# Walking the columns of float32r matmuls in steps of four 16-byte lines, with operands moved to other start addresses

## The chip, the cores and the metric

The kernel runs on one core of a Trainium2 chip. The metric is the device time of one execution in microseconds (us). Three runs of the kernel before gave 803.9, 803.96 and 804.22 us; the median is 803.96 us.

## What is computed

The reference is an attention with a sigmoid in place of the softmax, followed by a channel mix:

```python
scores = scale * np.matmul(q, k.transpose(0, 1, 3, 2)) - np.log(S)
attn = 1.0 / (1.0 + np.exp(-scores))
x = np.matmul(attn, v)                       # then laid out as [batch, seq, 768]
x_prev = x shifted by one position, zeros first
xk = mu_k * x + (1.0 - mu_k) * x_prev
xr = mu_r * x + (1.0 - mu_r) * x_prev
k = np.maximum(xk @ w_k, 0.0)
out = sigmoid(xr @ w_r) * ((k * k) @ w_v)
```

There are 8 batches, 12 heads of 64 dimensions, 448 positions, 768 channels and 1024 hidden channels. The inputs are float32, some of the weights float64.

## The kernel before, in words

**Number formats.** TensorE multiplies float32 as it is, or as float32r, a shorter form that streams one column a cycle. Where the kernel uses float32r it splits each operand into a rounded part (hi) and the remainder (lo) and adds three products, hi by hi, lo by hi and hi by lo, in PSUM. ScalarE or VectorE makes the hi part by a copy, VectorE the lo part by a subtraction.

**Attention** (the first 246 us) walks over 48 pairs of heads, two pairs to a round. For each pair and each 128-row chunk of keys, `scores` (line 348) issues the three float32r products (`kh`, `kl` are the keys, `qh`, `ql` the queries), each as two matmuls, one for each head of the pair, in the upper and the lower 64 rows of the array (line 361). The keys are the stationary operand, whose weights are loaded, and the queries the moving operand, whose 448 columns are streamed. The very first chunk is done in plain float32. `score_tails` (line 372) does the last 64 keys in float32, in four 64x64 tiles of the array at once. `sigmoid` (line 383) takes the scores out of PSUM on ScalarE. `weigh` (line 395) and its relatives multiply by the values in float32, also in four 64x64 tiles (lines 402 and 426), and `gather` (line 432) makes the two mixes of x and writes them to DRAM.

**Channel mix** (from 246 us to the end) has three stages, R_ (w_r), K_ (w_k) and V_ (w_v). Each is a Strassen-like scheme of seven products in place of eight, over four sets of columns (`PAIRS`, line 562): three of 512 columns and one of 256. `convert_seven` (line 269) has made the seven combinations of the weights from float64 on VectorE while attention ran; they stand in `slots`, hi and lo. `operand` (line 587) makes the hi and lo parts of the moving operands, in the tiles `rr` and, reused from attention, `qh` and `ql`. `multiply` (line 646) issues the products, with line 670 as the one matmul instruction; every matmul loads 128 columns of weights of its own and streams 512 or 256 columns into one PSUM bank. `evacuate` and `finish` take the results out.

**Order of the work.** A planner (`Plan`, line 24) lists all operations with an engine, an assumed cost and a priority, simulates the engines, and writes the instructions out in the order of the simulated starts. DMAs go out on SyncE's queue, a few on ScalarE's.

**Addresses.** SBUF tiles are laid out one behind the other by `ring` (line 174), and `gap` (line 177) leaves bytes free between them. Per partition, counted from a multiple of 256 bytes: `slots`, `rr`, and everything behind them up to `wexpo` start at 224; `kn` and `vn` at 160; `qn`, `qh` and `ql` at 224; `kh` and `kl` at 160; `pf` and all behind it at 224. So the weights of the scores start 64 bytes lower than the queries that stream past them, and the weights of the products (pieces of 512 bytes of `slots`) at the same distance from a multiple of 256 as the streams.

Of the kernel before, what the change touches and what calls it, by code (L numbers as in the profile page):

```python
# [23 lines left out]
class Plan:  # L24
# [9 lines left out]
    def op(self, engine, cost, prio, run, reads, writes, dma=None, gate=False, opens=None):  # L34
        i = len(self.ops)
        deps = set()
        for r in reads:
            if r in self.writer:
                deps.add(self.writer[r])
        for w in writes:  # L40
            if w in self.writer:
                deps.add(self.writer[w])
            deps.update(self.readers.get(w, ()))
        for r in reads:
            self.readers.setdefault(r, []).append(i)
        for w in writes:
            self.writer[w] = i
            self.readers[w] = []
        deps.discard(i)
        self.ops.append(Op(engine, cost, prio, run, deps, dma, gate, opens))  # L50
# [58 lines left out]
def attention_then_channel_mix(  # L109
# [15 lines left out]
    nc = tc.nc  # L125
    P = 128
# [40 lines left out]
    WK_PACE, WV_PACE = 1.5, 1.5  # L167
    CAST_DVE = lambda n, a: n % 2 == 1 or n == 2

    WHOLE = 1  # L170
    ZEROS = 336
    Q_FIRST = 256

    def ring(pool, name, bufs, shape, dtype):
        return [pool.tile(shape, dtype, name=f"{name}{i}") for i in range(bufs)]

    def gap(pool, name, size):
        pool.tile([P, size // 4], F32, name=name)

    base = ctx.enter_context(tc.tile_pool(name="base", bufs=1, side="left"))  # L180
    apool = ctx.enter_context(tc.tile_pool(name="apool", bufs=1, side="right"))
# [2 lines left out]
    pscore = psc.enter_context(tc.tile_pool(name="pscore", bufs=1, space=PSUM, side="right"))  # L184

    slots = ring(base, "slot", 7, [P, 2 * WO], F32R)
    rr = ring(base, "rr", 6, [P, 2, T], F32R)
    ys = ring(base, "ys", 3, [P, T], F32)
    wraw = ring(base, "wraw", 2, [P, WP, 2], U32)
# [5 lines left out]
    vnr = ring(apool, "vn", 5, [P, T], F32)  # L195
    gap(apool, "gap1", 64)
    qnr = ring(apool, "qn", RAW, [P, T], F32)
    qhr = ring(apool, "qh", LEAD, [P, T], F32R)
    qlr = ring(apool, "ql", LEAD, [P, T], F32R)
    gap(apool, "gap2", 192)  # L200
    kh = ring(apool, "kh", LEAD, [P, KW], F32R)
    kl = ring(apool, "kl", LEAD, [P, KW], F32R)
    gap(apool, "gap3", 64)
    pfr = ring(apool, "pf", PFB, [P, 2, T], F32)
    ptr = ring(apool, "pt", PTB, [P, 2, T], F32)
    xxr = ring(apool, "xx", 2, [P, T], F32)
# [8 lines left out]
    sc = ring(pscore, "sc", 3, [P, 2, 512], F32)  # L215
# [8 lines left out]
    def mm(n, cols):  # L224
        return n * (cols / 2.4 + 13.4)

    def act(n, sbuf=False, ptr=False):
        return 100 + 0.834 * n + 42 * sbuf + 93 * ptr

    def dve(n, fast=False, ptr=False):  # L230
        return 135 + n / (1.92 if fast else 0.96) + 61 * ptr
# [37 lines left out]
    def convert_seven(w, t, half_rows, n, pace, at, put):  # L269
# [32 lines left out]
        combine(sub, s4, a12, s2, at + 3 * pace)  # L302
        put(2, s4, at + 3 * pace)

    def to_slot(t, n):
        def put(p, a, at):
            g = POS[p]
            hi, lo = (slots[g][:, half * KT[R_] * n + t * n:half * KT[R_] * n + (t + 1) * n] for half in range(2))
            K = ("slot", g, t)
            op(ACT, act(n, True), at, lambda: nc.scalar.copy(hi, a[0]), [a[1]], [K], gate=True)  # L310
            op(DVE, dve(n), at, lambda: nc.vector.tensor_sub(lo, a[0], hi), [a[1], K], [K + ("lo",)])
        return put
# [18 lines left out]
    def prepare(n, at):  # L331
        i = n % LEAD
        k0 = WHOLE * P if n == 0 else 0
        for src, hi, lo, a, w in ((kn[n % RAW][:, k0:KW], [t[:, k0:] for t in kh], [t[:, k0:] for t in kl], "k", KW - k0), (qn[n % RAW], qh, ql, "q", S)):
# [6 lines left out]
    half = [slice(h * D, (h + 1) * D) for h in range(2)]  # L341

    def pe(cost, go, reads, writes, at, opens=None):
        op(PE, cost, at, go, reads, writes + ["order"], opens=opens)
# [3 lines left out]
    def scores(n, c, u, at):  # L348
        i, m = n % LEAD, n % RAW
        mark = (n, c) in ((N - 1, 1), (N - 2, 2), (N - 1, 2))  # L350
        if n == 0 and c < WHOLE:
            pairs, cost, reads = ((knr[m], qnr[m]),), 752, [("kn", m), ("qn", m)]
        else:
            pairs, cost = ((kh[i], qhr[i]), (kl[i], qhr[i]), (kh[i], qlr[i])), 602
            reads = [(a, i) for a in ("kh", "kl", "qh", "ql")]

        def go(lo, hi):
            for e, (kk, qq) in enumerate(pairs):
                for h in range(2):
                    w = T if mark and e == len(pairs) - 1 else hi  # L360
                    nc.tensor.matmul(sc[u][:, h, lo:w], kk[half[h], c * P:(c + 1) * P], qq[half[h], lo:w], start=e == 0, stop=e == len(pairs) - 1, skip_group_check=mark)  # L361

        keys = [("sc", u, 0), ("sc", u, 1)]
        if (n, c) == (0, 0):

            pe(cost * Q_FIRST / S, lambda: go(0, Q_FIRST), reads, keys, at)
            pe(cost * (1 - Q_FIRST / S), lambda: go(Q_FIRST, S), reads + [("qn", 0, 1)], keys, at)
            return
        pe(cost + 2 * SWITCH * (n % 2 == c == 0), lambda: go(0, S), reads, keys, at)
# [91 lines left out]
    for t in range(KT[R_]):  # L461
        convert_seven(w_r, t, KT[R_], CW[R_], WR_PACE, WR_FROM + 4 * WR_PACE * t + 0.4, to_slot(t, CW[R_]))
# [68 lines left out]
    e = N % RAW  # L531
# [109 lines left out]
    def slot_keys(g):  # L641
        return [("slot", g, h) + x for h in range(3) for x in ((), ("lo",))]
# [3 lines left out]
    def multiply(stage, s, p, i, at, cols=slice(0, T), b=None, turn=0):  # L646
        g = POS[p]
        b = b or (yb if p in (5, 6, 3) else xb)[i]
        c = cols.stop - cols.start
        rs_ = used[stage, s, p]  # L650
        w = CW[stage]
        small = PAIRS[s][1] < T

        def go():
            n = len(rs_)

            def left(t, a):
                return slots[g][:, a * n * w + t * w + i * P:a * n * w + t * w + (i + 1) * P]

            if small:  # L660

                a = turn ^ (p in (1, 6, 3))
                terms = [(left(t, a), r[0], (T, SMALL)[a]) for t, r in enumerate(rs_)]
            else:
                terms = [(left(t, a), r[e][:, cols], c) for t, r in enumerate(rs_) for a, e in ((0, 0), (0, 1), (1, 0))]
            for e, (l, r, m) in enumerate(terms):
                nc.tensor.matmul(b[0][:, :m], l, r[:, :m], start=bool(p in (0, 4) and e == turn == 0), stop=e == len(terms) - 1 and bool(turn or not small), skip_group_check=True)  # L670

        cost = mm(len(rs_), (T, SMALL)[turn ^ (p in (1, 6, 3))]) if small else mm(3 * len(rs_), c)
        op(PE, cost, at, go, [k for r in rs_ for k in r[2:]] + slot_keys(g), [b[1]])
# [87 lines left out]
    for step, (stage, s, p) in enumerate(steps):  # L761
# [6 lines left out]
        small = PAIRS[s][1] < T  # L768
        for i in range(rows if small else 0):
            multiply(stage, s, p, i, at + unit * i / (2 * rows))  # L770
        for i in range(rows):
# [9 lines left out]
            if step == len(steps) - 3 and i == rows - 1:  # L781
                a, b = yb[i], yb[NFH - 1]
# [45 lines left out]
```

## Time and profile before

| | |
|---|---|
| median of three runs | 803.96 us |
| span of the profiled execution, first to last instruction | 801.9 us |
| TensorE matmul busy | 797.8 us, 99% |
| TensorE weight loads busy | 598.8 us, 75% |
| VectorE busy | 639.7 us, 80% |
| ScalarE busy | 496.0 us, 62% |
| mean DMA rate | 224 GB/s |

The span is that of one profiled execution; the runs' times, taken without a profile, are 2.1 us above it at the median. In the profile PE is TensorE's matmuls, PEld its weight loads, DVE VectorE, ACT ScalarE, POOL GpSimd. Matmuls follow each other in a pipeline, and the duration listed for one reaches into the next ones; the distance between two starts is what one of them takes of the time. In the timeline equal instructions that follow each other are merged into one row, with their number behind the x.

### The profile page before, as it was taken

The page shows a single profiled execution, that of the slowest core. Times are in us where ns is not written, and L with a number is a line of the kernel's source. Part 1 is how long each engine was busy: PE and PEld are TensorE (multiplying, and loading weights), DVE is VectorE, ACT ScalarE, POOL GpSimd, SP SyncE. Part 2 cuts the span into 40 slices and gives each one's busy share as a digit, 9 for nine tenths or more (in the row PEclk, how much of TensorE's full clock was granted, in tenths as well). Part 3 has the DMA queues.
Part 4 walks back from the last instruction along what each step waited for, and adds up shares of the span by engine and source line. Part 5 has one row for each costly group of instructions (what it writes and reads, how often), then busy time and mean ns, then how long its engine had stood idle before and what let it go on. Part 6 is the DMA issues. An engine that isn't in the chain of part 4 may idle for free.

```text
span 801.9 us, 14343 instructions
## 1 busy us (share of the span) xinstructions
PE 797.8 (99%) x4935; PEld 598.8 (75%) x4935; DVE 639.7 (80%) x1210; ACT 496.0 (62%) x870; POOL 2.9 (0%) x33
## 2 busy tenths in 40 slices
PE   9999999999999999999999999999999999999998
PEld 5555555555556888888888888888888888888887
DVE  4889888898898998899987974668597585677955
ACT  6788888877785555568766464567773434345431
POOL 0000000000000000000000000000000000000000
PEclk9999999999999999999999999999999999999999
DMA  8977978789887967668877772445775564457505
GB/s 276 282 262 243 304 242 275 254 274 340 295 293 272 313 236 218 228 238 257 277 243 223 243 256 87 162 151 155 226 243 179 172 184 131 132 166 253 186 23 176
DMA packets 105336, 179.74 MB, mean 224 GB/s; under 512 B 11952, under 2 KB 58800, under 8 KB 105264
## 3 DMA queue, kind: packets, MB, share of 16 engines
q1 hardware_dynamic: 104976, 178.61, 68.9%
q8 instruction: 39, 0.64, 0.3%
q14 instruction: 33, 0.27, 0.1%
q10 hardware_dynamic: 288, 0.23, 0.1%
HBM read 109.06 MB, written 69.73 MB: 223 GB/s over the span
## 4 chain that ended last, share of the span: by engine, by line
PE 99%; DVE 0%; issue 0%
PE pb L670 69%; PE av L402 13%; PE sc L361 10%; PE sc L376 2%; PE av L426 2%; PE av L361 2%; PE av L412 1%; PE sc L445 0%; DVE vn L720 0%
## 5 line engine op out<-in xcount | busy, mean ns | idle before, releaser
L670 PE MATMUL pb<-rr,slot 128*128 128x512 f32 (+1 forms) x1908 | 440.3, 379 | 0.0
L670 PEld LDWEIGHTS pb<-rr,slot 128*128 128x128 f32 x1908 | 348.0, 188 | 68.5 <-issue 0.8
L670 PE MATMUL pb<-qh,slot 128*128 128x512 f32 (+1 forms) x468 | 154.7, 374 | 0.0
L402 PE MATMUL av<-pf,vn 64*64 64x448 f32 x1104 | 118.1, 540 | 0.0
L391 ACT ACTIVATE pf<-sc 128x896 f32<-128x896 f32 x120 | 104.0, 962 | 0.5 <-PE sc L361 0.5
L670 PEld LDWEIGHTS pb<-qh,slot 128*128 128x128 f32 x468 | 86.2, 188 | 15.8
L402 PEld LDWEIGHTS av<-pf,vn 64*64 64x64 f32 x1104 | 41.4, 132 | 56.9 <-issue 36.1
L670 PE MATMUL pb<-ql,slot 128*128 128x512 f32 (+1 forms) x177 | 68.4, 387 | 0.0
L594 ACT CAST rr<-ys 128x512 fp32r<-128x512 f32 (+1 forms) x56 | 30.9, 568 | 35.7 <-PE pb L670 34.1
L361 PE MATMUL sc<-qh,kh 64*128 64x448 f32 x238 | 46.2, 384 | 0.0
L728 ACT COPY pb<-pb 128x512 f32<-128x512 f32 x40 | 22.6, 575 | 34.5 <-PE pb L670 31.5
L361 PE MATMUL sc<-ql,kh 64*128 64x448 f32 (+1 forms) x238 | 43.4, 361 | 0.0
L436 ACT COPY xx<-av 128x448 f32<-128x448 f32 x48 | 23.3, 539 | 32.3 <-PE av L402 26.5
L361 PE MATMUL sc<-qh,kl 64*128 64x448 f32 x238 | 43.2, 359 | 0.0
L437 DVE TENSOR_TENSOR dx<-xx 128x448 f32<-128x448 f32 x48 | 29.9, 623 | 16.6 <-ACT xx L436 16.4
L595 DVE TENSOR_TENSOR rr<-pf,rr 128x512 fp32r<-128x512 f32 (+1 forms) x40 | 23.0, 608 | 20.5 <-ACT rr L594 20.5
L670 PEld LDWEIGHTS pb<-ql,slot 128*128 128x128 f32 x177 | 33.2, 188 | 6.7
L595 DVE TENSOR_TENSOR rr<-ys,rr 128x512 fp32r<-128x512 f32 (+1 forms) x56 | 33.6, 620 | 3.4 <-ACT rr L594 3.1
L361 PEld LDWEIGHTS sc<-qh,kh 64*128 64x128 f32 x238 | 22.4, 185 | 18.5 <-issue 15.5
L595 DVE TENSOR_TENSOR rr<-vn,rr 128x512 fp32r<-128x512 f32 (+1 forms) x48 | 29.6, 626 | 7.7 <-ACT rr L594 7.4
L594 ACT CAST rr<-vn 128x512 fp32r<-128x512 f32 (+1 forms) x48 | 26.9, 571 | 10.4 <-PE pb L670 8.8
L639 DVE TENSOR_TENSOR slot<-pf,slot 128x768 fp32r<-128x768 f32 x28 | 26.8, 956 | 7.8 <-ACT slot L638 7.6
(160 smaller groups left out, 1071.8 us busy)
## 6 DMA issues: line engine op xcount, KB each, us to landing
vn<-in_v SPq DMA_DIRECT2D x48, 224.0 KB, 4.3
xr_d<-mr SPq DMA_DIRECT2D x48, 224.0 KB, 4.5
xk_d<-mk SPq DMA_DIRECT2D x48, 224.0 KB, 4.3
kn<-in_k SPq DMA_DIRECT2D x47, 224.0 KB, 3.9
qn<-in_q SPq DMA_DIRECT2D x47, 224.0 KB, 4.2
wraw<-in_moe_w_k SPq DMA_DIRECT2D x12, 512.0 KB, 5.8
wraw<-in_moe_w_v SPq DMA_DIRECT2D x16, 384.0 KB, 3.7
k_d<-pt SPq DMA_DIRECT2D x23, 256.0 KB, 3.1
```

The costliest lines, as they stand in the source:

```text
L361: nc.tensor.matmul(sc[u][:, h, lo:w], kk[half[h], c * P:(c + 1) * P], qq[half[h], lo:w], start=e == 0, stop=e == len(pairs) - 1, skip_grou ...
L376: nc.tensor.matmul(sc[u][half[m % 2], h, :S], kn[m % RAW][half[h], KW:], qn[m % RAW][half[h], :], start=True, stop=True)
L391: op(ACT, 815, at, lambda: nc.scalar.activation(f, sc[u][:, :, :S], AF.Sigmoid, bias=NEG_LOG_S, scale=SCALE), R, K, opens=opens)
L402: nc.tensor.matmul(av[m % 2][half[h], :w], vn[m % 5][half[r], h * NC + c, :], pfr[(m * NC + c) % PFB][half[r], h, :w], start=(turn, c) == ...
L426: nc.tensor.matmul(av[r][half[h], :w], vn[(n + h) % 5][half[r], 2 * NC, :], ptr[n // 2 % PTB][half[r], h, :w], start=False, stop=stop, ski ...
L436: op(ACT, act(S), at - 1, lambda: nc.scalar.copy(x[:, 1:], av[n % 2][:, :S]), [AV[n % 2]], [X])
L437: op(DVE, dve(S), at, lambda: nc.vector.tensor_sub(d, x[:, 1:], x[:, :S]), [X], [G])
L594: op(ACT, act(w, True), at, lambda: nc.scalar.copy(hi, y[:, :w]), [Y], [H], gate=True)
L595: op(DVE, dve(w), at, lambda: nc.vector.tensor_sub(lo, y[:, :w], hi), [Y, H], [L])
L639: op(DVE, dve(n), at, lambda hi=hi, lo=lo, w=w: nc.vector.tensor_sub(lo, w, hi), W + [K], [K + ("lo",)])
L670: nc.tensor.matmul(b[0][:, :m], l, r[:, :m], start=bool(p in (0, 4) and e == turn == 0), stop=e == len(terms) - 1 and bool(turn or not sma ...
L728: op(ACT, act(T), at, lambda: nc.scalar.copy(y(), x()), [X], [Y])
```

## The change

Every float32r matmul of line 361 and all of line 670 get another order of columns. A new helper, `by_lines`, rearranges the free dimension of an operand of n columns, seen as n/16 blocks of four lines of four columns, so that the first lines of all blocks come first, then the second lines, and so on. A line is four float32 columns, 16 bytes. The moving operand and the PSUM output of a matmul are rearranged alike, so each column's result lands where it did before. In the instruction a read of 512 consecutive columns becomes one of 4 times 32 runs of 4 columns. Weights are read as before. The float32 matmuls (the first chunk of scores, the tails and the products with the values) are not touched.

Gaps move four groups of tiles. `rr`, `ys` and the tiles of the weight conversion move from 224 to 0 bytes past a multiple of 256, `qh` and `ql` as well, and `kh` and `kl` from 160 to 224. `slots`, `kn`, `vn`, `qn`, `pf` and all behind `pf` stay. So in scores and in products the weights now start 32 bytes below a multiple of 256, and the streams on one.

The planner's costs are not touched, and every engine's instructions stand in the order of before.

```diff
--- before.py
+++ after.py
@@ -167,6 +167,7 @@
     WK_PACE, WV_PACE = 1.5, 1.5
     CAST_DVE = lambda n, a: n % 2 == 1 or n == 2
 
+    LINE = 4
     WHOLE = 1
     ZEROS = 336
     Q_FIRST = 256
@@ -184,6 +185,7 @@
     pscore = psc.enter_context(tc.tile_pool(name="pscore", bufs=1, space=PSUM, side="right"))
 
     slots = ring(base, "slot", 7, [P, 2 * WO], F32R)
+    gap(base, "gap0", 32)
     rr = ring(base, "rr", 6, [P, 2, T], F32R)
     ys = ring(base, "ys", 3, [P, T], F32)
     wraw = ring(base, "wraw", 2, [P, WP, 2], U32)
@@ -195,12 +197,12 @@
     vnr = ring(apool, "vn", 5, [P, T], F32)
     gap(apool, "gap1", 64)
     qnr = ring(apool, "qn", RAW, [P, T], F32)
+    gap(apool, "gap5", 32)
     qhr = ring(apool, "qh", LEAD, [P, T], F32R)
     qlr = ring(apool, "ql", LEAD, [P, T], F32R)
-    gap(apool, "gap2", 192)
+    gap(apool, "gap2", 224)
     kh = ring(apool, "kh", LEAD, [P, KW], F32R)
     kl = ring(apool, "kl", LEAD, [P, KW], F32R)
-    gap(apool, "gap3", 64)
     pfr = ring(apool, "pf", PFB, [P, 2, T], F32)
     ptr = ring(apool, "pt", PTB, [P, 2, T], F32)
     xxr = ring(apool, "xx", 2, [P, T], F32)
@@ -302,6 +304,9 @@
         combine(sub, s4, a12, s2, at + 3 * pace)
         put(2, s4, at + 3 * pace)
 
+    def by_lines(t):
+        return t.rearrange("p (a b c) -> p b a c", b=4, c=LINE)
+
     def to_slot(t, n):
         def put(p, a, at):
             g = POS[p]
@@ -358,7 +363,10 @@
             for e, (kk, qq) in enumerate(pairs):
                 for h in range(2):
                     w = T if mark and e == len(pairs) - 1 else hi
-                    nc.tensor.matmul(sc[u][:, h, lo:w], kk[half[h], c * P:(c + 1) * P], qq[half[h], lo:w], start=e == 0, stop=e == len(pairs) - 1, skip_group_check=mark)
+                    out_, right_ = sc[u][:, h, lo:w], qq[half[h], lo:w]
+                    if len(pairs) > 1:
+                        out_, right_ = by_lines(out_), by_lines(right_)
+                    nc.tensor.matmul(out_, kk[half[h], c * P:(c + 1) * P], right_, start=e == 0, stop=e == len(pairs) - 1, skip_group_check=mark)
 
         keys = [("sc", u, 0), ("sc", u, 1)]
         if (n, c) == (0, 0):
@@ -667,7 +675,7 @@
             else:
                 terms = [(left(t, a), r[e][:, cols], c) for t, r in enumerate(rs_) for a, e in ((0, 0), (0, 1), (1, 0))]
             for e, (l, r, m) in enumerate(terms):
-                nc.tensor.matmul(b[0][:, :m], l, r[:, :m], start=bool(p in (0, 4) and e == turn == 0), stop=e == len(terms) - 1 and bool(turn or not small), skip_group_check=True)
+                nc.tensor.matmul(by_lines(b[0][:, :m]), l, by_lines(r[:, :m]), start=bool(p in (0, 4) and e == turn == 0), stop=e == len(terms) - 1 and bool(turn or not small), skip_group_check=True)
 
         cost = mm(len(rs_), (T, SMALL)[turn ^ (p in (1, 6, 3))]) if small else mm(3 * len(rs_), c)
         op(PE, cost, at, go, [k for r in rs_ for k in r[2:]] + slot_keys(g), [b[1]])
```

## Rows read from the trace of the kernel before

**Rows 1.** Page, parts 1 and 2: span; busy us, share, instructions; granted clock in tenths, 40 slices.

```profile
span 801.9 us, 14343 instructions
PE 797.8 (99%) x4935; PEld 598.8 (75%) x4935; DVE 639.7 (80%) x1210; ACT 496.0 (62%) x870; POOL 2.9 (0%) x33
...
PEclk9999999999999999999999999999999999999999
```

**Rows 2.** Page, part 4: the chain that ended last, by engine and line.

```profile
PE 99%; DVE 0%; issue 0%
PE pb L670 69%; PE av L402 13%; PE sc L361 10%; PE sc L376 2%; PE av L426 2%; PE av L361 2%; PE av L412 1%; PE sc L445 0%; DVE vn L720 0%
```

**Rows 3.** Waits, engine PE: releaser; us in total, times, longest.

```profile
PE sc L445 <- PEq L798: 0.8, 1, 0.8
```

**Rows 4.** Chain in order of time: start us, us, what.

```profile
246.29 552.32 PE pb L670 x2553
```

**Rows 5.** Groups by form, PE, whole span: count | busy us, mean ns | idle before.

```profile
L670 PE MATMUL pb<-rr,slot 128*128 128x512 f32 x1722 | 414.0, 389 | 0.0
L670 PE MATMUL pb<-qh,slot 128*128 128x512 f32 x403 | 141.3, 389 | 0.0
...
L670 PE MATMUL pb<-ql,slot 128*128 128x512 f32 x173 | 67.3, 389 | 0.0
...
L670 PE MATMUL pb<-rr,slot 128*128 128x256 f32 x186 | 29.3, 283 | 0.0
...
L670 PE MATMUL pb<-qh,slot 128*128 128x256 f32 x65 | 13.8, 283 | 0.0
...
L670 PE MATMUL pb<-ql,slot 128*128 128x256 f32 x4 | 1.1, 283 | 0.0
```

**Rows 6.** Timeline, PE and PEld, 300 to 304 us: start us, length us, what.

```profile
299.66 4.70 PE L670 MATMUL pb<-rr,slot 128*128 128x512 f32 x20
...
299.89 4.27 PEld L670 LDWEIGHTS pb<-rr,slot 128*128 128x128 f32 x19
```

**Rows 7.** Timeline, PE and PEld, 796.2 to 799 us.

```profile
796.27 0.28 PE L670 MATMUL pb<-qh,slot 128*128 128x256 f32 x1
...
796.99 0.88 PE L670 MATMUL pb<-rr,slot 128*128 128x256 f32 x6
797.71 0.28 PE L670 MATMUL pb<-qh,slot 128*128 128x256 f32 x1
...
797.71 0.19 PEld L670 LDWEIGHTS pb<-ql,slot 128*128 128x128 f32 x1
```

**Rows 8.** Timeline, PE, 53.2 to 57.5 us: scores of one pair.

```profile
56.62 0.36 PE L361 MATMUL sc<-qh,kl 64*128 64x448 f32 x2
...
57.42 0.36 PE L361 MATMUL sc<-ql,kh 64*128 64x448 f32 x2
```

**Rows 9.** Timeline, PE, the same stretch: float32 products.

```profile
53.19 0.93 PE L376 MATMUL sc<-qn,kn 64*64 64x448 f32 x8
53.94 2.44 PE L402 MATMUL av<-pf,vn 64*64 64x448 f32 x24
```

**Rows 10.** Groups by form, PE, 338.4 to 338.55 us: 256 columns behind a 512.

```profile
L670 PE MATMUL pb<-qh,slot 128*128 128x256 f32 x2 | 0.4, 283 | 0.0
L670 PE MATMUL pb<-rr,slot 128*128 128x256 f32 x1 | 0.3, 277 | 0.0
```

**Rows 11.** Groups by form, PE, 338.6 to 338.8 us: 512 columns behind two 256s.

```profile
L670 PE MATMUL pb<-rr,slot 128*128 128x512 f32 x1 | 0.4, 396 | 0.0
```

**Rows 12.** Groups by form, PE, 798.5 to 799 us: the last matmul.

```profile
L670 PE MATMUL pb<-qh,slot 128*128 128x256 f32 x1 | 0.3, 279 | 0.0
```

**Rows 13.** Windows: stretch, length, busy us (x) of PE, PEld, DVE, ACT, POOL; PEclk, DMA share, GB/s.

```profile
50.00:100.00 50.00, 49.97 (x500) 27.97 (x500) 44.72 (x93) 40.89 (x63) 0.49 (x5) 1.00 0.83 270
250.00:450.00 200.00, 200.00 (x912) 166.63 (x911) 178.55 (x326) 125.15 (x237) 0.00 (x0) 1.00 0.76 249
```

## The prediction

> **What bounds the kernel now.** I read the busy shares and the granted clock first. TensorE is busy for 797.8 of 801.9 us and its clock stands at the top digit in all 40 slices [rows 1]; the stage rows give 1.00, so the engine is at the upper of its two levels, 2.4 GHz. The chain that ended last is TensorE for 99%, and 69% of the span is the products of line 670 [rows 2]. TensorE's own waits come to 0.8 us, all at the start [rows 3]. In the chain in order of time the products are one unbroken piece of 552.32 us [rows 4]. So nothing that another engine does is on the path: the time is the number of matmuls by the time from the start of one to the start of the next. A matmul's listed duration (379 ns and the like) overlaps its neighbours and is no price. I read prices from the timeline, as distances between starts.
>
> *Products.* 2298 of them have 512 columns and 255 have 256 [rows 5]. Twenty of 512 columns in a row fill 4.70 us; without the last one's 0.39 that is 19 steps in 4.31 us, 226.8 ns a step [rows 6]. At 2.4 GHz and one column a cycle 512 columns are 213.3 ns, so 13.5 are over. From 796.27 to 797.71 us there are twelve of 256 columns: 120.0 ns a step, over 106.7, again 13.3 over [rows 7]. **The excess belongs to the matmul, not to its columns.** Over the whole stretch: 2298 x 213.33 + 255 x 106.67 = 517.4 us, 552.3 - 517.4 = 34.9, or 13.7 ns for each of 2553.
>
> *Scores in float32r.* Two 64-row matmuls run side by side; four pairs start between 56.62 and 57.42 us, 200 ns a pair against 186.7 for 448 columns: 13.3 over [rows 8]. There are 858 such matmuls, 429 pairs: 5.7 us. *Plain float32 products* (lines 376, 402) run four 64x64 tiles at once: 8 of them, two groups, from 53.19 to 53.94 us, 375 ns a group [rows 9]. That is 448 columns at two cycles each (373.3 ns) and under 2 ns over. **At half the reading pace the excess is all but gone, so it is no fixed price of changing weights.**
>
> *What the 13 ns go with.* A weight load is listed as 0.19 us and starts with the matmul before its own [rows 6, 7]. Beside 512 columns it lies inside one matmul; beside 256 columns its tail lies over its own. If loading slows streaming, the shares must shift where the two lengths meet, and they do. The first 256 after a 512, whose own weights were already in, lasts 277 ns where the next ones last 283 [rows 10]; the first 512 after 256s, which carries a tail as well as the next load, lasts 396 where 389 is usual [rows 6, 11]. The very last matmul has no load after it: 279 in place of 283 [rows 12]. The tail costs 6 to 7 ns, the head 4: about 10 ns of the 13.5 are paid while weights are read, and some 3.5 are left, near the float32 groups' 2.
>
> **The change, part by part.** *Order.* No instruction is added, removed or moved on any engine; counts, waits and DMAs stay. What changes is the order in which 2553 + 858 matmuls walk their columns, and four groups of addresses.
>
> *Moving operand, read as lines 0, 4, 8, ... and then 1, 5, 9, ...* All matmuls of the trace of before read consecutive columns, so it holds no price for this. Bounds: nothing gained (the conflict is one of capacity, every weight line costs a slot of the stream), or all 40.6 us (34.9 + 5.7). Between them stands the loads' measured share, 10 ns: if the reordered stream no longer meets the weights, 2553 x 10 + 429 x 10 = **29.8 us**. I take that value, as it rests on the rows nearest to the case: the same matmul with and without a load beside it [rows 10 to 12]. Why I think that the order can do it: two ascending streams of consecutive lines are read at once and delay each other by the same amount in products, where both start 224 bytes past a multiple of 256, and in scores, where the weights start 64 bytes lower. A shift of the start doesn't matter when both streams walk every line in turn; steps of four lines are another walk, in which they can keep out of each other's way. This is an inference; no row shows it.
>
> The rule that speaks against the change: the Trainium skill, "TensorE: Matmul & The Clock Gate", section "Step-by-step: what each phase is for", says that TensorE has two independent SBUF read ports, and that loading the next weights steals nothing from the running matmul's reads. By that rule the whole excess would be a fixed cost and the sum would be 0. The trace disagrees: 277, 283, 389 and 396 ns follow the loads.
>
> *Output, written in the same runs of four.* Nothing in the trace of before writes so. I cost it at 0; the far bound is a whole 2.4 GHz cycle for each of 128 runs (53.3 ns a product, see the rivals).
>
> *Addresses.* Slots stay 224 bytes past a multiple of 256; moving operands go to 0; keys of the scores go from 160 to 224, so that scores and products now have the same 32 bytes between weights and stream. With consecutive reading, products at distance 0 and scores at 64 pay 13.5 and 13.3 [rows 6, 8], so the shift alone is costed at 0; its bound is those 0.2 ns, 0.6 us either way. Scratch of the weight conversion moves by 32 bytes: 0, since no step waits for it [rows 3].
>
> *What a faster TensorE meets.* The closest cover is VectorE, with 178.55 of 200 us between 250 and 450 us [rows 13]. Products 10 ns shorter make that stretch about 191 us, and VectorE 93% busy. No capacity is exceeded, but operands come later relative to the matmuls. I charge **1 us** (bounds 0 and 3, a third of the stretch's 9 us). In attention VectorE does 44.72 of 50 us [rows 13], and TensorE gets only 4.3 us (429 x 10 ns) shorter over 240: nothing.
>
> *Sum.* 29.8 - 1 = 28.8 saved from 801.9: 773.1 us of span. The median of the runs is 803.96, 2.1 us above the span (execution outside it), so **775 us**.
>
> **The rivals.**
> *A. No change (within 0.2%, which is what a measurement of this kernel can tell from none: 1.6 us).* Weights and stream share something that one alone can use, whichever line it asks for. For: the excess is the same 13.3 to 13.7 ns at both distances and for 64-row pairs, as a fixed number of slots would be. Against: nothing, until other walks have been measured. 804 us.
> *B. Half of it.* Some lines still meet: 5 ns instead of 10 go, 14.9 us: 789 us. For: weights still pass every line. Faster too.
> *C. Slower: runs of four cost the output or the read a cycle each.* Place: the 128 run ends of each product (112 of a score). Price: 53.3 x 2298 + 26.7 x 255 + 46.7 x 429 = 149 us; with the 29.8 gained, 923 us. It decides from 10 / 128 = 0.08 ns a run, a fifth of a cycle: below that the change wins, and a whole cycle loses by far. For: every matmul in the trace writes consecutive columns, so it would not have shown. Against: with four columns to each line, as many lines are touched as before. The Trainium skill, "PSUM — Partial Sum Buffer", section "Specifications (TRN2)", says that any non-contiguous access slows matmuls significantly; its lines there are 8 bytes, of which each run fills two whole ones. No run here shows it yet.
> *D. Slower: the streams meet more often.* A step of 64 bytes repeats the same few places, and a load that falls into step with them is delayed at every line. Twice the share now: 10 ns more a matmul, 834 us. Against: the chosen 32 bytes between weights and stream differ from both distances of before.
>
> **How the numbers follow.** Forecast, the loads' share gone (from 8 to all 13.7 ns): 0.46. B: 0.17. Together faster by over 0.2%: 0.63. A: 0.17. C: 0.10 and D: 0.10, so slower: 0.20. The forecast's own range runs from all 40.6 us gone (763) to 8 ns with 3 us given back (783); little speaks for its low end, as float32 groups keep 2 ns: I cut at 766. To hold 8 in 10 the range must take in B and A: 766 to 806. C and D stay outside.
>
> **What would show it.** Right: a run of twenty 512-column products has steps near 216 to 218 ns, 256-column ones near 110, score pairs near 190; the products are one piece of about 527 us; durations no longer differ by 6 or 7 ns where 512 and 256 columns meet; no wait of TensorE over 1 us in 250 to 450. A: steps still 227. C: steps of 260 and more whether or not a load lies beside them. D: steps of 230 to 240, and a last matmul far shorter than its neighbours. Wrong in a way not listed: steps shorten, but TensorE begins to wait for operands.

## The result and the profile after

The changed kernel takes 795.41 us, the median of four runs (795.01 to 799.65), against 803.96 before: a ratio of 0.9909 with a 95% interval of 0.9885 to 0.9932. It is faster, by 8.5 us and not by the 28.8 that were forecast. The profiled execution is the slowest of the four, 799.65 us with a span of 797.5.

The page after, its head and the chain that ended last (before: [rows 1, 2]):

```profile
span 797.5 us, 14360 instructions
...
PE 793.1 (99%) x4935; PEld 598.8 (75%) x4935; DVE 639.3 (80%) x1210; ACT 495.9 (62%) x870; POOL 2.9 (0%) x33
...
PEclk9999999999999999999999999999999999999999
...
PE pb L678 68%; PE av L410 14%; PE sc L369 10%; PE sc L384 2%; PE av L434 2%; PE av L369 2%; PE av L420 1%; DMA qn<-in_q 0%; DVE vn L728 0%; ACTq L244 0%
```

TensorE bounds the kernel as before, at the same clock. Its chain in order of time, start and length in us, and pieces of the same chain in three stretches of some 60 and 30 us, where a row's length by its count is the mean step from one product to the next (the line is now 678):

```profile
1.16 3.58 DMA qn<-in_q
...
248.12 88.42 PE pb L678 x396
336.56 457.68 PE pb L678 x2157
379.95 60.17 PE pb L678 x267
559.95 60.16 PE pb L678 x267
749.88 30.14 PE pb L678 x137
```

The products take 546.1 us in place of 552.3 [rows 4], 6.2 less; this execution gives 1.8 back at its start, where the first load of queries lands later (products begin at 248.12, not 246.29). Steps are 225.3 ns in the first two stretches and 220.0 in the last, against 226.7 in the same view of before:

```profile
559.78 60.29 PE pb L670 x266
```

In a long stretch of 512 columns every product of the kernel before lasts the same; now not. Line 670 and line 678 in the stretch from 600 to 606 us, durations in ns as minimum/median/maximum, before:

```profile
L670 PE MATMUL pb<-rr,slot x28: 389/389/389, 599.7 to 605.9; 128*128 128x512 f32 x28
```

and after:

```profile
L678 PE MATMUL pb<-rr,slot x28: 380/385/393, 599.7 to 605.8; 128*128 128x512 f32 x28
```

Read from the starts in the trace, the steps repeat in a cycle of five (222, 219, 230, 224, 232 ns) up to a stretch of 256-column products behind 700 us, and from there in one of three (221, 221, 218). The first has steps well over the 226.7 of before, and neither has the forecast's mean of 216 to 218. Read likewise, products of 256 columns take 114.6 or 115.7 ns in place of 119.7, not the 110 that were forecast. The scores gained nothing: sixteen pairs take 3.25 us here, 203 ns each.

```profile
58.39 0.35 PE L369 MATMUL sc<-qh,kl 64*128 64x448 f32 x2
...
61.64 0.37 PE L369 MATMUL sc<-ql,kh 64*128 64x448 f32 x2
```

Before, the same sixteen, from 56.62 us [rows 8] to the last below, took 3.21 us, 201 ns each:

```profile
59.83 0.36 PE L361 MATMUL sc<-ql,kh 64*128 64x448 f32 x2
```

TensorE's waits have grown by 0.3 us, at the start; none stands in the products:

```profile
PE sc L453 <- PEq L806: 0.8, 1, 0.8
PE sc L369 <- DMA qn<-in_q: 0.3, 1, 0.3
```

### The profile page after: what moved, and what is told of

Its sections match the earlier page's. It is cut to its first block, busy times and chain, and to the rows that moved or that the text cites. A ratio compares the mean times of both kernels' runs of the same rounds, so it can differ in the third digit from the quotient of the medians.

```text
span 797.5 us, 14360 instructions
## 1 busy us (share of the span) xinstructions
PE 793.1 (99%) x4935; PEld 598.8 (75%) x4935; DVE 639.3 (80%) x1210; ACT 495.9 (62%) x870; POOL 2.9 (0%) x33
## 4 chain that ended last, share of the span: by engine, by line
PE 99%; DMA 0%; DVE 0%; ACTq 0%; issue 0%
PE pb L678 68%; PE av L410 14%; PE sc L369 10%; PE sc L384 2%; PE av L434 2%; PE av L369 2%; PE av L420 1%; DMA qn<-in_q 0%; DVE vn L728 0%; ACTq L244 0%
## 5 line engine op out<-in xcount | busy, mean ns | idle before, releaser
L678 PE MATMUL pb<-rr,slot 128*128 128x512 f32 (+1 forms) x1908 | 435.4, 375 | 0.0
L678 PE MATMUL pb<-qh,slot 128*128 128x512 f32 (+1 forms) x468 | 152.9, 370 | 0.0
L399 ACT ACTIVATE pt<-sc 128x896 f32<-128x896 f32 x24 | 22.1, 920 | 18.0 <-PE sc L384 18.0
```

Of the source, the lines that this page charges most:

```text
L399: op(ACT, 815, at, lambda: nc.scalar.activation(f, sc[u][:, :, :S], AF.Sigmoid, bias=NEG_LOG_S, scale=SCALE), R, K, opens=opens)
L678: nc.tensor.matmul(by_lines(b[0][:, :m]), l, by_lines(r[:, :m]), start=bool(p in (0, 4) and e == turn == 0), stop=e == len(terms) - 1 and ...
```

## The experiments

Theory M: weight loads and the stream delay each other when they ask for SBUF lines that get in each other's way; how often depends on the walk, the distance of the start addresses and the phase between the two. Rivals: S, a load takes fixed slots of the stream, whichever lines are asked for; W, runs of four cost something in the output. "Distance" is stream start minus weight start, modulo 256 bytes. Steps are those of 512-column products, unless another length is named. Where no range is given with a time, it is that of a single run.

### The changed kernel again, and its two parts alone

The changed kernel without an edit:

> The changed kernel once more. Theory M (weight loads and the stream meet in lines of SBUF, and how often depends on the walk, on the distance of their start addresses and on their phase): the step from one 512-column product to the next was not one number in the changed kernel but a repeating cycle of five (222, 219, 230, 224, 232 ns, mean 225.4) until about 740 us and a cycle of three (221, 221, 218, mean 220) behind it, and three of its four runs were 4 us faster than the profiled one. So the phase decides, and another execution may spend more or less of the products in the cycle of three: a product piece between 562 and 540 us, time 790 to 800. Rival S (each weight line takes a fixed slot of the stream, the gain came from elsewhere): the same steps at the same places, 795 to 800.

Measured: 794.35 us (793.53 to 797.56). The chain from 380 and from 560 us:

```profile
380.00 60.17 PE pb L678 x267
559.83 60.28 PE pb L678 x274
```

The cycle of 220.0 ns began at the second stretch of 256-column products, some 200 us earlier than in the first profile, and the products took 542.0 us. So two executions of one program differ in where the cycle changes, which S did not allow; that the phase of load and stream is behind it is M's reading, which this run does not show.

The walk alone (the gaps of before put back):

```diff
-    gap(base, "gap0", 32)
-    gap(apool, "gap5", 32)
-    gap(apool, "gap2", 224)
+    gap(apool, "gap2", 192)
...
+    gap(apool, "gap3", 64)
```

> Only the walk in steps of four lines; all addresses as in the kernel before (weights and streams of the products at the same distance from a multiple of 256, weights of the scores 64 bytes lower). Theory M: the distance decides how often the streams meet, so the steps of products differ from both kernels; anything from 217 to 235 ns, and not the cycle of five of the changed kernel. Rival S: the walk alone makes the gain, the addresses nothing: steps as in the changed kernel, 795 us.

Measured: 797.33 us (795.48 to 798.67), ratio 0.9921 (0.9904 to 0.9939).

```profile
379.85 60.30 PE pb L677 x270
559.85 60.29 PE pb L677 x266
```

Steps of 223.3 and 226.7, cycles that the changed kernel does not have. The addresses alone (no `by_lines`):

```diff
-nc.tensor.matmul(by_lines(b[0][:, :m]), l, by_lines(r[:, :m]),
+nc.tensor.matmul(b[0][:, :m], l, r[:, :m],
...
```

> Only the addresses of the changed kernel, columns read in order. Both theories: two streams of consecutive lines meet equally often at any distance, so steps of 226.8 ns for products and 200 ns for score pairs as before, 804 us. If M holds for consecutive reading too, the steps move by some ns with the distance.

Measured: 819.37 us, 16 slower than before; steps of 233.3 ns:

```profile
559.81 60.20 PE pb L678 x258
```

Both expectations were wrong here, mine the more. For consecutive reads, too, the addresses decide: distance 32 costs 6.6 ns a 512-column product more than 0 (those of 256 columns, read from the starts, fall from 119.7 to 116.7). S falls, and so does a step of the prediction. The two parts of the change pull against each other: at distance 32 the walk takes 8 to 13 ns away, of which the move to that distance had added 6.6.

### Reads or writes, and the floor

The walk in the reads alone:

```diff
-nc.tensor.matmul(by_lines(b[0][:, :m]), l, by_lines(r[:, :m]),
+nc.tensor.matmul(b[0][:, :m], l, by_lines(r[:, :m]),
...
```

> The changed kernel with the walk in the reads alone; results are written to consecutive columns, so the columns of scores and products stand in another order than they should. Theory M (weight loads and stream meet in lines of SBUF): all the effect is in the reads, so 512-column products have the steps of the changed kernel, cycles of mean 225.3 or 220.0 ns, and score pairs about 201. Rival W (runs of four in PSUM cost something, which eats most of the gain): steps fall to about 217.

Measured: 793.17 us, steps of 225.3, from the second stretch of 256 columns on 220.0, exactly the changed kernel's:

```profile
559.87 60.28 PE pb L678 x274
```

And the walk in the output alone, the other way round:

> The changed kernel with the walk in the PSUM output alone and consecutive reads, so again the columns stand in another order. M: steps as with the addresses alone, 233.4 ns. W: longer than that, by what the runs of four cost in the output (the changed kernel's 225 against the 217 that I forecast would make 8 ns: 241).

Measured: 819.46 us, steps of 233.3, those of consecutive reads at these addresses:

```profile
559.90 60.20 PE pb L678 x258
```

W falls: runs of four in the output cost nothing here. The rule of the Trainium skill ("PSUM — Partial Sum Buffer", "Specifications (TRN2)") that any non-contiguous access slows matmuls does not show for runs of 16 bytes: 233.3 ns with and without them.

A stream that stays on one line, in the kernel before:

```diff
+one = r[:, :4].rearrange("p (a c) -> p a c", a=1).to_broadcast([P, m // 4, 4])
-nc.tensor.matmul(b[0][:, :m], l, r[:, :m],
+nc.tensor.matmul(b[0][:, :m].rearrange("p (a c) -> p a c", c=4), l, one,
...
```

> The kernel before, in which every product reads the first line (four columns) of its stream over and over instead of its 512 or 256 columns, so the products' values are wrong; counts, weights, lengths and outputs stay. Theory M (weight loads and stream meet in lines): a stream that stays on one place meets each weight load only where the load passes that place, so steps fall from 226.8 to the floor that is left without meetings, 214 to 218 ns; products about 520 us in all. Rival S (a load takes slots of the stream, whichever lines it asks for): 226.8 as before. If asking for the same place again and again is itself slow, steps are far longer than 227.

Measured: 776.61 us, steps of 215.8 ns with the same loads beside them:

```profile
559.86 60.22 PE pb L671 x279
```

This is the least of all runs here: 10.8 ns of the 13.3 over 512 columns go when the stream asks for no new lines, though every load is still there. No run shows whether a line that is asked for again is fetched anew at all. The Trainium skill ("TensorE: Matmul & The Clock Gate", "Step-by-step: what each phase is for") has two independent read ports, by which a load takes nothing from the stream's reads. The traces disagree: the last product of the kernel before, with no load beside it, is 4 ns shorter than its neighbours [rows 12], and a score pair changes from 203 to 197.5 ns when its weights, the keys, are moved alone (mix, below).

Half the weights, in the kernel before (the first term of each group whole):

```diff
+wd = P if e == 0 else P // 2
-nc.tensor.matmul(b[0][:, :m], l, r[:, :m],
+nc.tensor.matmul(b[0][:wd, :m], l[:, :wd], r[:, :m],
...
```

> The kernel before, with 64 in place of 128 columns of weights in every product but the first of each group of terms: half of the sums of those products are left out, the number of matmuls and their streams stay. Theory M and rival S: what a load costs goes by its lines, so half a load costs 5 ns in place of 10: steps of about 222 ns, the product piece about 12 us shorter (nine of ten matmuls by 5 ns). A fixed price of each matmul (my reading that 3.5 ns is fixed and 10 is not, wrong): steps of 226.8 and the time of before.

Measured: 810.09 us, steps of 229.8:

```profile
560.00 60.22 PE pb L671 x262
```

A miss for every theory: a shorter load made products longer. Loads of two lengths may shift the phase, and half of the array's columns stay unused; this run cannot tell which of the two counts, if either. It shows only that the price does not go by a load's length.

### Other distances, steps and runs

All are the changed kernel with some numbers changed: `gap0`, `gap5` and `gap2` for the distance (g160, g224, g128), `b` in `by_lines` for the step (b2, b8), `LINE` for the length of a run (c8), or both (b2c8).

> The changed kernel with streams of products and scores starting 128 bytes above their weights (modulo 256) in place of 32. M: with the walk, too, the distance decides: steps differ from 225.3 and 220.0, by several ns in either direction. Rival S2 (the walk's gain is the same at any distance, only consecutive reads depend on it): cycles of the changed kernel, 220 to 225.3.

> The changed kernel with steps of eight lines (128 bytes) in place of four, at the same addresses. M: another walk, another number of meetings; the steps of products differ from 225.3 and 220.0. If the lines lie in places that repeat after 256 bytes, steps of 128 bytes alternate between two of them and weight lines meet the stream either seldom or in long runs: from 216 to 235 ns. S2: any walk that leaves consecutive lines gains the same, 220 to 225.

Measured: distance 128, 803.08 us, nearly the time of the kernel before (803.93 on that chip); its chain from 380 and 560 us:

```profile
379.82 60.26 PE pb L678 x262
559.82 60.40 PE pb L678 x268
```

230.0 and 225.4 ns. Steps of 128 bytes, 857.64 us, from 380 and 620 us (at 560 this slower kernel still has 256-column products among the others):

```profile
379.91 60.25 PE pb L678 x243
619.94 60.25 PE pb L678 x243
```

247.9 in both. S2 falls for both.

> The changed kernel with steps of two lines (32 bytes) in place of four, same addresses. After steps of eight gave 248 ns and steps of one (addresses alone) 233.4, four being 220 to 225: if the meeting depends on how many places the stream goes round before it returns (M), two lies between one and four or near four: 222 to 230 ns. S2 (any walk short of eight is as good as four): 220 to 225.

> The changed kernel with streams of products and scores 32 bytes below their weights (distance 224 modulo 256), walk of four. M: distance matters with this walk too (at 0 products took 223.3 or 226.6 by turns, at 32 220.0 or 225.3, at 128 225.3 or 230): another pair of values between 218 and 231, with no rule yet for which. If even and odd multiples of 32 make the difference, 224 behaves as 32 does: 220 and 225.3.

> The same at distance 160. If even and odd multiples of 32 make the difference, as 32: 220 and 225.3. If nearness of the starts does, nearer to 128: 225 to 230.

Measured: b2 818.57 us and 233.3 ns, as if the columns were read in order, which nobody expected; g224 801.54 us and 226.7; g160 800.08 us and 226.2. The chains of b2 and g160:

```profile
559.87 60.20 PE pb L678 x258
559.90 60.17 PE pb L678 x266
```

That even and odd multiples of 32 make the difference is refuted; 160 lies nearer to 128, as the other reading had it, but on one row alone. Of the five distances tried with the walk of four, 32 is the best for products.

> The changed kernel in runs of eight columns (two lines) and steps of 128 bytes, same addresses. If the step decides (128 bytes gave 248 ns with runs of one line): well over 233. If it is how often the same place is asked for again at once (runs of one line at 128 bytes come back to a place after two lines, runs of two after four): below 233.

> The changed kernel in runs of two lines and steps of 64 bytes. If the step decides (64 bytes: 220 to 225): 220 to 225. If the length of the run does: between the walk of one-line runs (220 to 225) and consecutive reading (233.4): 226 to 232.

Measured: c8 812.03 us and 230.0 ns, below 233, so its step of 128 bytes alone does not decide; b2c8 819.02 us and 233.3, neither of the two ways. Of the two lengths of run tried, steps of 64 bytes help only with the one-line run.

### What sets the cycle, and a better version

Kick, an odd step put in (the first 512-column product of each step as two of 256):

```diff
+parts = [(0, m // 2), (m // 2, m)] if i == 0 and e == 0 and m == T else [(0, m)]
+for f, t in parts:
+    nc.tensor.matmul(by_lines(b[0][:, f:t]), l, by_lines(r[:, f:t]),
...
```

> The changed kernel, with the first 512-column matmul of every step issued as two of 256 columns (one more load and some 8 ns in each of 63 steps, 0.5 us in all). In three profiles the products went from the cycle of 225.3 ns to that of 220.0 at a stretch of 256-column matmuls and never back. Theory P (the phase with which 512-column products resume sets the cycle, and 220.0 keeps itself): the odd steps re-draw the phase early, so the cycle of 220.0 is reached within the first steps: product piece about 538 us, 787 to 791 us, with less spread between runs. Rival Q (the cycle is set by something that changes in the course of the program, such as other engines' traffic): 225.3 until the middle as before, 794 to 800.

Measured: 794.09 us (793.68 to 795.03); 84 products were split, not 63. Products began in the cycle of 220.0 and, from about 515 us on, went over to that of 225.3, but for a short stretch near 710. Durations as above, from 400 and from 600 us:

```profile
L680 PE MATMUL pb<-rr,slot x17: 379/381/382, 399.8 to 405.9; 128*128 128x512 f32 x17
L680 PE MATMUL pb<-rr,slot x12: 380/385/393, 600.6 to 604.5; 128*128 128x512 f32 x12
```

So 220.0 does not keep itself, against P, and 225.3 did not last until the middle, against Q; nothing was gained. That the split draws the phase anew is not shown: the next kernel begins at 220.0 without it.

Mix, the scores back at distance 64, products as in the changed kernel:

```diff
-    gap(apool, "gap2", 224)
+    gap(apool, "gap2", 192)
...
+    gap(apool, "gap3", 32)
```

> The changed kernel with the keys of the scores 64 bytes below their streams (modulo 256) in place of 32; products as in the changed kernel. In the kernel with the walk alone score pairs took 197.1 ns at this distance against 201 to 203 in the changed kernel. If distance sets it for scores too: pairs of about 197, 429 x 4 to 6 ns = 2 us less than the changed kernel, 793 us. If it was the phase and not the distance: 201 to 203, 795.

Measured: 792.5 us (790.92 to 794.45). Sixteen score pairs take 3.16 us, 197.5 ns each:

```profile
46.53 0.36 PE L370 MATMUL sc<-qh,kl 64*128 64x448 f32 x2
...
49.69 0.35 PE L370 MATMUL sc<-ql,kh 64*128 64x448 f32 x2
```

Over all of attention the median step between pairs is 195 ns in both profiles of this version, and 201 to 203 in the three of the changed kernel. Only the keys were moved, so the stream by itself does not decide it; the walk alone, at the same distance from other starts of both, has a median of 194. So the distance sets it for scores. For products only the stream was ever moved, and no run there tells the distance from the stream's own start. This version's products begin at 220.0 ns, pass to 225.3 at the first stretch of 256-column products and return at the second:

```profile
249.78 50.38 PE pb L679 x229
379.89 60.16 PE pb L679 x267
559.88 60.28 PE pb L679 x274
```

Both versions on one chip, timed side by side:

> The changed kernel, timed beside the next one on the same chip. Cycles drawn by chance between 225.3 and 220.0 ns, at the start of the products and at each stretch of 256-column matmuls: 792 to 800 us, median about 795.

> The changed kernel with scores at distance 64. Pairs of 197 to 198 ns in place of 201 to 203, so about 2 us below the changed kernel's median (429 pairs by 3.5 to 5.3 ns), with the same spread from the products' cycles: median about 793.

Measured: the changed kernel 793.78 us (792.88 to 797.23), ratio 0.9879 (0.9863 to 0.9896); mix 790.26 us (790.01 to 790.8), ratio 0.9831 (0.9818 to 0.9845). The intervals do not meet: mix beats both kernels, by 13.7 and 3.5 us. The two profiled executions (797.23 and 790.05 us) differ by 7.2: 1.0 lies in attention (products begin at 244.69, not 245.73), 2.0 in the first piece of the products, which mix begins in the cycle of 220.0, and 4.1 in the rest:

```profile
245.73 88.42 PE pb L678 x396
334.18 457.68 PE pb L678 x2157
```

for the changed kernel, and for mix:

```profile
244.69 86.37 PE pb L679 x396
331.09 453.56 PE pb L679 x2157
```

At most the 1.0 is the scores' own; the products are the same in both, and what they gain is their cycle's. Both profiles of mix begin them at 220.0 and all three of the changed kernel at 225.3. Whether the place of the keys brings that about is not shown.

## Why the prediction was right and wrong

*Right:* TensorE alone bounds the kernel before and after. Most of the 13.3 ns over a product's columns hangs on which lines the stream asks for beside its loads: the stream of one line loses 10.8. The output's runs cost nothing, and no operand came late, so the 1 us charged for VectorE was not spent. The sign came out, in part by luck: with the same walk at distance 128 the one run took 803.08 us, and nothing in the prediction told the two distances apart.

*A reading that does not hold:* I put the 10 ns together from a tail of 6 to 7 and a head of 4. But the trace of before has more [rows 11]: behind the 256s at 338 us the steps are 233, 236, 228, 233 and 231 ns before they settle, and of these five products only the first carries a tail. Durations of the fourth and fifth, where 389 is usual:

```profile
L670 PE MATMUL pb<-rr,slot 128*128 128x512 f32 x2 | 0.6, 394 | 0.0
```

So 396 is not the price of one tail; an odd step is felt for several products. That 10 lies close to 10.8 is luck in part, and the longer steps with half the weights fit neither.

*Wrong, first step:* "if the reordered stream no longer meets the weights, 2553 x 10 + 429 x 10 = 29.8 us". The term was mis-sized, and its condition not met: a 512-column product loses 1.3 ns of its 226.7 in one cycle and 6.7 in the other, not 10; a score pair loses nothing. In place of 29.8 us the products gave 6.2 in the first profile and 10.3 in the second, the scores 0. I had bounds of 0 and 40.6 and chose the full measured share, because it was the value whose row I had; that row said what loads cost, and nothing of what a new walk would save. Rival B, half of it (789 us), was the nearer.

*Wrong, second step:* "A shift of the start doesn't matter when both streams walk every line in turn", with 0.6 us as its bound. It rested on two distances that happen to cost the same; the third costs a product 20 ns over its columns where they cost 13, and the addresses alone make the kernel 16 us slower. This also hid that the new distance is good for products and poor for scores, which the change gave one distance: with the walk a score pair takes 197.5 ns at 64 and 203 at 32, a product less at 32 than at 0.

*Rivals.* A falls with the addresses alone. C falls with the walk in the output alone and, for the read, with steps below those of before. D's slowing shows with steps of 128 bytes (247.9 ns), not with the steps of 64 for which it was written.

What stays open: by which rule loads and stream get in each other's way; that it is their lines that meet is argued. Five distances, three steps and two lengths of run give no rule that I could state. Open too is what decides the cycle after a stretch of 256-column products. It is no even chance: in the profiles of the changed kernel, of the walk in the reads alone and of mix, six in all, the unbroken run of 714 products from about 350 us has 225.3 and the last, of 252, has 220.0. The 780 between them had either.

## What to carry to other kernels

A fixed excess per matmul over its columns can be hindrance between weight loads and the stream: look for durations that shift where matmuls of two lengths meet, and see with a stream that stays on one line how much there may be to win. That is no forecast for a reordering; it must be tried, and each distance of start addresses with it, for each kind of matmul by itself. Two equal readings at two addresses don't show that addresses don't matter.

## What the runs showed of the hardware that was not expected

At distance 32 and in runs of one line, reading in steps of 32 bytes costs a 512-column product as much as reading in order (233.3 ns), in steps of 64 8 to 13 ns less, in steps of 128 15 more (247.9). In the changed kernel products of equal form at equal addresses settle in one of two cycles, 225.3 or 220.0 ns a step. They change only where 256-column products come between: no unbroken run of 512s, the longest of 780, changed its cycle. So the products of two executions of one program differ by 4.1 us (546.1 and 542.0) with no wait of TensorE among them. The kernel before, at distance 0 and read in order, always settles at 226.7 ns, and its runs on one chip lie within 0.7 us.
